# One PSUM bank per projection unit from the seventh on, the last x block asked for earlier, the folded weights later

## The chip, the core and the metric

The kernel runs on one core of a Trainium2 chip. The metric is the device time of one execution in microseconds (us), as the median of several runs. The core has five engines that each run their own instruction stream in order and meet through semaphores: TensorE (PE) for matmuls, VectorE (DVE), ScalarE (ACT), GpSimd (POOL), and SyncE (SP), which here only issues DMA transfers. Matmuls write to PSUM, which has eight banks of 128 partitions x 512 float32; ACT and DVE read it from there.

## The reference

Two attention branches read the same x (2048 tokens, width 448, 16 heads of 28), and a gate per token mixes their outputs:

```python
g = sigmoid((x * gate_w).sum(-1, keepdims=True))
a = A_ref(x, A_wqkv, A_w_phi, A_wo)   # linear attention, Hedgehog feature map
b = B_ref(x, B_wqkv, B_wo)            # softmax attention
return g * a + (1 - g) * b

# A: q, k, v = split(x @ wqkv)
pq, pk = q @ w_phi, k @ w_phi                       # per head
phi_q = concat([softmax(pq), softmax(-pq)])         # phi_k the same of pk
num = phi_q @ (phi_k^T @ v); den = phi_q @ sum(phi_k) + 1e-6
a = (num / den) @ wo

# B: q, k, v = split(x @ wqkv)
p = softmax(q @ k^T * 28**-0.5)
b = (p @ v) @ wo
```

## The kernel before

All matmuls take float32 operands that are split into a high part (rounded to the PE's fp32r format) and a low part (the rest); a product is the sum of high x high, high x low and low x high. The last of the four 128-row blocks of x and of its weights holds only 64 rows, and its other 64 rows carry the low part, so that a projection takes 11 matmuls: three for each of the first three blocks, two for the last (`x3`, L110).

The part that the change touches is the front of the kernel: the q and k projection of branch B. `UNITS` (L554) lists 28 units (m, t): m is a block of 128 of the 896 q and k columns, t a block of 512 of the 2048 tokens. Units 0 to 3 (t = 0) are computed together in `first_units` (L605), as their inputs arrive. Units 4 to 19 follow one by one in the loop at L646, and the last eight are spread over the next stage. `proj_qk` (L559) takes a PSUM bank, runs the 11 matmuls, and `keep_qk` (L568) evicts the result: ACT writes the high part into a tile `ev` (four buffers in rotation), DVE subtracts it to get the low part, and SP stores both to the scratch tensor `qk_d` in DRAM.

A unit's bank comes from `later` as long as that list has entries, then from `ps_s`, a rotation of three single banks (tag "s"; units 0 to 2 hold them first). The entries of `later` are halves of two pair tiles `pr[0]` and `pr[1]` from `ps_mx` (two banks each, tag "mx"), which the max units use later on.

What else goes on in that loop, by the unit number n:

- x comes in four blocks of 512 tokens. `x_loads(t)` issues two transfers of two 128-row blocks each into staging tiles (`stg`, three buffers in rotation, which the weights' loads share); `splits(n + 1)` calls `split_x`, in which ACT writes the high part of both halves to `XH`, and DVE and POOL the low parts. Block 2 is split at n=4, block 3 at n=8, each ahead of that unit's own eviction. The units of block 3 begin with n=12.
- `phi` and the transposed k weights of branch A (`wkAT`, four transfers, `load_fold` at L375) are loaded; `fold` (L382) multiplies them, eight small matmuls for each of four groups, into a bank of the same `ps_s` rotation, and ACT and DVE evict the result into `wkA_s`. `load_fold` begins with a one-row copy on POOL that reads `phi_s` and orders the loads behind it. All four folds are needed by the first `pk` projection of the next stage.
- `wB1`, the weights of units 16 and up, is loaded at n=10 and split at n=12 and n=14.
- `pair_query` and `pair_load` read parts of `qk_d` back (tiles qp, kp, kt; ten transfers for the first pair); POOL forms differences of the keys from them (`take_subs`, at n=14 and 19). From n=16 on `mx_unit` (L258), which looks for the largest score of each query, runs ahead of each unit: four small matmuls into two pair tiles, one ACT and two DVE instructions.

PE, DVE, ACT and POOL run in the order in which the program writes their instructions. The order of SP's queue is set by a planner that picks among the transfers that it expects to be ready, the earlier in the program first; so SP's order can differ from the program's.

Of the kernel before, what the change touches and what calls it, by code (L numbers as in the profile page):

```python
# [34 lines left out]
def f32(ap):  # L35
    return ap.bitcast(F32)
# [3 lines left out]
def gated_mix_kernel(ctx, tc, xT, wqkB, wvB, wvA, wkAT, wqAT, phi, woA, woB,  # L40
# [20 lines left out]
    def ps_s(nm):  # L61
        return ps.tile([P, 512], F32, tag="s", name=nm, bufs=psn[0])

    def ps_pv(nm):
        return ps.tile([P, 512], F32, tag="pv", name=nm, bufs=1)

    def ps_mx(nm, d):
        return ps.tile([P, 2, 512], F32, tag="md" if d and psn[1] == 3 else "mx", name=nm,
                       bufs=1 if d and psn[1] == 3 else 2)
# [29 lines left out]
    def weights(place, nm):  # L99
        if place == 1:  # L100
            return wp.tile([P, 2, 4, 512], F32R, tag="w1", name=nm)
        if place == 2:
            return front.tile([P, 2, 4, D], F32R, tag="w2", name=nm)
        return wp.tile([P, 2, 4, 450], F32R, tag="w3", name=nm)
# [31 lines left out]
    def take_lows():  # L136
        while lows:
            lows.pop(0)()
# [25 lines left out]
    def take_acts():  # L164
        while acts:
            acts.pop(0)()

    def take_subs():
        while subs:
            subs.pop(0)()  # L170
# [35 lines left out]
    def pair_load(g, c):  # L206

        hp, b = divmod(c, 2)
        heads = (2 * hp, 2 * hp + 1)
        r = mx_tile("kc", f"kp{g}_{c}", 5)  # L210
        t = mx_tile("kd", f"kt{g}_{c}", 1)
        mx_rows(r, (0, 1), k_d[g], heads, b * 1024)
        mx_rows(r, (2, 3), k_d[g], heads, b * 1024 + 512)
        mx_rows(t, (2, 3), k_d[g], heads, b * 1024)
        mxs[("kp", g, c)] = r

        def sub():
            for i in (2, 3):
                js = slice(32 * i, 32 * i + DH)
                nc.gpsimd.tensor_sub(r[js], f32(r[js]), f32(t[js]))  # L220

        subs.append(sub)

    def pair_query(gq, hp):
        g, qb = divmod(gq, NQ)
        mxs[("qp", gq, hp)] = mx_rows(mx_tile("qc", f"qp{gq}_{hp}", 3), range(4), q_d[g],
                                      (2 * hp, 2 * hp + 1) * 2, qb * 512)
# [127 lines left out]
    def load_x(t, b):  # L355
        return stage(2, 512, xT[:, b:b + 2, t * 512:(t + 1) * 512], f"xraw{t}_{b}")
# [18 lines left out]
    def load_fold(src, nm):  # L375
        wts[nm] = bk.tile([112, NG, 512], F32, tag="wt", name=f"wt{nm}", bufs=1)
        if nm == "k":
            nc.gpsimd.tensor_copy(wts[nm][:1, :, 0], phi_s[:1, :, 0])
        for k in range(NG):
            nc.sync.dma_start(wts[nm][:, k, :], src[:, k, :])  # L380

    def fold(dst, nm, g, b0=0, n=4):  # L382

        wt = wts[nm][:, g, :]
        pw = ps_s(f"pw{nm}{g}_{b0}")
        for b in range(n):
            nc.tensor.matmul(pw[:, b * 112:(b + 1) * 112], wt[:, (b0 + b) * P:(b0 + b + 1) * P],
                             phi_s[:, g, :], start=True, stop=True)
        pw3 = pw[:, :n * 112].rearrange("p (b f) -> p b f", f=112)
        bs, gs = slice(b0, b0 + n), slice(g * 112, (g + 1) * 112)  # L390
        nc.scalar.copy(dst[:, 0, bs, gs], pw3)
        nc.vector.tensor_sub(dst[:, 1, bs, gs], pw3, f32(dst[:, 0, bs, gs]))
# [166 lines left out]
    def proj_qk(n, ev):  # L559

        m, t = UNITS[n]
        tt = slice(t * 512, (t + 1) * 512)
        pq = later.pop(0) if later else ps_s(f"pqk{t}_{m}")
        w, c = wB[m // 4], m % 4 * P
        run(pq, [(w[:, i, b, c:c + P], x) for b, x, i in x3(tt)])
        keep_qk(m, t, pq, ev)

    def keep_qk(m, t, pq, ev):  # L568
        tt = slice(t * 512, (t + 1) * 512)
        e = ev.tile([P, 2, 512], F32R, tag="ev", name=f"ev{t}_{m}")  # L570
        nc.scalar.copy(e[:, 0, :], pq)  # L571
        nc.vector.tensor_sub(e[:, 1, :], pq, f32(e[:, 0, :]))  # L572
        nc.sync.dma_start(qk_d[m * P:(m + 1) * P, :, tt], f32(e))
# [7 lines left out]
    wkA_s = weights(2, "wkA_s")  # L581
# [3 lines left out]
    def loads(key, *fns):  # L585
        raws[key] = [f() for f in fns]

    def x_loads(t):
        loads(("x", t), lambda: load_x(t, 0), lambda: load_x(t, 2))

    def part_loads(key, src, n, nm):
        loads(key, lambda: load_part(src, n, nm, 0), lambda: load_part(src, n, nm, 2))

    def split_part(w, key, n, i, low=nc.vector):
        split_weight(w, raws[key][i], slice(2 * i, 2 * i + 2), slice(0, n), low)

    def splits(n):

        if n % 4 == 1 and n < 12:
            split_x(n // 4 + 1, raws.pop(("x", n // 4 + 1)))  # L600
        if n in (13, 15):
            split_part(wB[1], "wB1", 384, (n - 13) // 2)
        take_lows()

    def first_units():  # L605

        raw = [stg.tile([P, 2, 512], F32, tag="stg", name=f"first_raw{b}") for b in range(3)]
        raw.append(f32(ev.tile([P, 2, 512], F32R, tag="ev", name="first_raw3")))
        for b in range(4):
            nc.sync.dma_start(raw[b][:, 0, :], wqkB[:, b, :512])  # L610
            nc.sync.dma_start(raw[b][:, 1, :], xT[:, b, :512])
        x_loads(1)
        pqs = [ps_s(f"pqk0_{m}") for m in range(3)] + [ps_pv("pqk0_3")]
        pr = [ps_mx(f"pqk_{i}", False) for i in range(2)]
        later.extend((pr[0][:, 0, :], pr[1][:, 0, :], pr[0][:, 1, :]))
        for _ in range(8):
            nc.tensor.matmul(pqs[3][:, :P], ident, ident, start=True, stop=True)
        for b in range(4):
            w, x = wB[0][:, :, b, :], XH[:, b, :512]
            nc.scalar.copy(w[:, 0, :], raw[b][:, 0, :])  # L620
            (nc.scalar.copy if b else nc.vector.tensor_copy)(x, raw[b][:, 1, :])
            nc.vector.tensor_sub(w[:, 1, :], raw[b][:, 0, :], f32(w[:, 0, :]))
            if b < 3:
                nc.vector.tensor_sub(XL[:, b, :512], raw[b][:, 1, :], f32(x))
                todo = [(0, x), (1, x), (0, XL[:, b, :512])]
            else:
                nc.vector.tensor_sub(x[64:], raw[b][64:, 1, :], f32(x[64:]))
                todo = [(0, x), (1, x)]
            if b < 3:
                order = [(i, m) for i in range(3) for m in range(4)]  # L630
            else:
                order = [(i, m) for m in range(4) for i in range(2)]
            for i, m in order:
                nc.tensor.matmul(pqs[m], w[:, todo[i][0], m * P:(m + 1) * P], todo[i][1],
                                 start=b == 0 and i == 0, stop=b == 3 and i == 1,
                                 skip_group_check=True)
        hold = raws[("x", 1)][0][:1, 0, :4]
        splits(1)
        nc.gpsimd.tensor_copy(phi_s[:1, :, 0], hold)
        for m in range(4):  # L640
            keep_qk(m, 0, pqs[m], ev)

    later = []
    first_units()
    pkv = ps_pv("pkv")
    for n in range(4, NP):  # L646
        take_acts()
        if n in (4, 6):
            x_loads(n // 2)
        if n == 5:  # L650
            nc.sync.dma_start(phi_s, phi)
            load_fold(wkAT, "k")
        if n == 10:
            part_loads("wB1", wqkB[:, :, 512:896], 384, "wB1")
        splits(n + 1)
        if n == 14:
            part_loads("wvA", wvA, 450, "wvA")
            nc.sync.dma_start(sel_s, sel)
            nc.sync.dma_start(mask_s, mask)
            for v in vap:  # L660
                nc.gpsimd.memset(v[:, :, 28:32], 0.0)
                nc.gpsimd.memset(v[:, :, 28:29], 1.0)
        if 16 <= n < 20:
            mx_unit()
        proj_qk(n, ev)
        if n in (16, 18):
            split_part(wvA_s, "wvA", 450, (n - 16) // 2)
            take_lows()
        if n in (10, 12, 14, 17):
            fold(wkA_s, "k", {10: 0, 12: 1, 14: 2, 17: 3}[n])  # L670
        if n == 10:
            pair_query(0, 0)
            pair_load(0, 0)
        if n == 15:
            pair_load(0, 1)
            pair_query(0, 1)
        if n in (14, 19):
            take_subs()
# [522 lines left out]
```

## Time and profile before

| | us |
|---|---|
| median of 3 runs | 1028.66 |
| lowest and highest of them | 1027.72 and 1028.92 |
| span of the profiled execution | 1027.1 |
| PE busy in it | 1018.7 (99%) |
| ACT busy in it | 819.4 (80%) |
| DVE busy in it | 672.8 (65%) |
| POOL busy in it | 245.1 (24%) |

The span runs from the first to the last instruction of one execution, the slowest (here the only) core's. PE's busy time is that of pipelined matmuls, so that 99% does not mean that PE works at its peak. PEld is PE's weight load, which overlaps its matmuls. In rows of waits, "A <- B: 2.3, 1, 2.3" says that A's engine sat idle for 2.3 us in total, once, at longest 2.3 us, until B ended. In rows of the timeline, neighbouring instructions of one kind are merged ("x4"), and their durations overlap where they are pipelined. "SPq" rows are the issuing of a transfer by SP, not the transfer itself.

### The profile page before, as it was taken

The page shows a single profiled execution, that of the slowest core. Times are in us where ns is not written, and L with a number is a line of the kernel's source. Part 1 is how long each engine was busy: PE and PEld are TensorE (multiplying, and loading weights), DVE is VectorE, ACT ScalarE, POOL GpSimd, SP SyncE. Part 2 cuts the span into 40 slices and gives each one's busy share as a digit, 9 for nine tenths or more (in the row PEclk, how much of TensorE's full clock was granted, in tenths as well). Part 3 has the DMA queues.
Part 4 walks back from the last instruction along what each step waited for, and adds up shares of the span by engine and source line. Part 5 has one row for each costly group of instructions (what it writes and reads, how often), then busy time and mean ns, then how long its engine had stood idle before and what let it go on. Part 6 is the DMA issues. An engine that isn't in the chain of part 4 may idle for free.

```text
span 1027.1 us, 17751 instructions
## 1 busy us (share of the span) xinstructions
PE 1018.7 (99%) x6344; PEld 561.2 (55%) x6344; DVE 672.8 (65%) x1335; ACT 819.4 (80%) x1534; POOL 245.1 (24%) x213
## 2 busy tenths in 40 slices
PE   8999999999999999999999999999999999999998
PEld 7878888878779433333333333333333333354545
DVE  5466566997750578888878788787878887710102
ACT  5354445687753899999999999999999999969672
POOL 1226456688436302111011110101201101011010
PEclk9999999999999999999999999999999999999999
DMA  8873110132245703233633123522313355414311
GB/s 294 292 243 116 42 34 19 43 90 79 91 129 122 158 19 83 65 71 68 127 70 77 46 66 81 129 57 50 87 46 74 87 131 138 124 56 127 122 42 54
DMA packets 64025, 98.88 MB, mean 96 GB/s; under 512 B 17952, under 2 KB 24720, under 8 KB 63936
## 3 DMA queue, kind: packets, MB, share of 16 engines
q1 hardware_dynamic: 63936, 97.74, 35.4%
q8 instruction: 50, 0.82, 0.4%
q14 instruction: 39, 0.32, 0.1%
HBM read 69.54 MB, written 27.78 MB: 95 GB/s over the span
## 4 chain that ended last, share of the span: by engine, by line
PE 95%; DVE 2%; DMA 1%; ACT 1%; issue 0%; SPq 0%; DVEq 0%; ACTq 0%
PE st L850 29%; PE pv L977 25%; PE pm L321 9%; PE pqk L108 5%; PE poa L108 4%; PE pk L126 4%; PE pva L126 4%; PE pob L108 3%; PE pq L108 3%; PE pvb L108 2%; PE pmb L284 2%; PE pvb L126 2%; PE pn L532 1%; PE pft L520 1%; PE pkv L475 1%; PE poL L1011 1%
## 5 line engine op out<-in xcount | busy, mean ns | idle before, releaser
L868 ACT ACTIVATE p<-st 128x512 f32<-128x512 f32 x1020 | 525.9, 609 | 29.5 <-PE st L850 27.8
L332 DVE TENSOR_REDUCE part<-pm 128x1 f32<-128x512 f32 x477 | 304.6, 685 | 131.5 <-PE pm L321 124.9
L850 PE MATMUL st<-qst,kst 128*128 128x512 f32 x1024 | 315.6, 430 | 0.5 <-ACT vb L694 0.5
L977 PE MATMUL pv<-p,vb 128*32 128x512 f32 x2048 | 272.8, 605 | 0.2 <-DVE oUb L398 0.2
L850 PEld LDWEIGHTS st<-qst,kst 128*128 128x128 f32 x1024 | 173.1, 187 | 137.4 <-issue 75.8
L321 PEld LDWEIGHTS pm<-kc,qc 28*128 28x128 f32 x848 | 40.5, 181 | 177.8 <-ACT p L868 169.4
L325 ACT ACTIVATE rl<-pm 128x512 f32<-128x512 f32 x212 | 126.9, 599 | 11.1 <-PE pm L321 0.3
L419 POOL TENSOR_TENSOR oUb<-oUb,rsb 128x512 f32<-128x512 f32 x15 | 19.4, 1291 | 469.2 <-DMA rsb<-rdb 375.1
L329 DVE CUSTOM_DVE_ANT_0 rl<-pm,rl 128x512 f32<-128x512 f32 x159 | 108.2, 680 | 0.0
L321 PE MATMUL pm<-kc,qc 28*128 28x512 f32 x848 | 107.1, 495 | 0.0
L289 DVE CUSTOM_DVE_ANT_0 rl<-pmb,rl 128x512 f32<-128x512 f32 x88 | 57.1, 686 | 32.4 <-ACT rl L287 32.4
L977 PEld LDWEIGHTS pv<-p,vb 128*32 128x32 f32 x2048 | 40.3, 108 | 67.6 <-issue 63.4
L988 DVE SCALAR_TENSOR_TENSOR acc<-pob,gate,acc 128x448 f32<-128x448 f32 x12 | 8.2, 683 | 86.2 <-PE pob L108 86.2
L108 PE MATMUL pqk<-XH,wB 128*128 128x512 f32 x192 | 60.8, 404 | 2.3 <-DVE ev L572 2.3
L287 ACT ACTIVATE rl<-pmd 128x1024 f32<-128x1024 f32 x44 | 45.3, 1029 | 8.0 <-ACT z_s L485 2.4
L571 ACT CAST ev<-pqk 128x512 fp32r<-128x512 f32 x28 | 16.0, 589 | 40.2 <-PE pqk L108 35.7
L108 PE MATMUL poa<-woA_s,oTa 128*128 128x448 f32 x192 | 43.2, 374 | 0.0
L108 PEld LDWEIGHTS pqk<-XH,wB 128*128 128x128 f32 x192 | 36.0, 192 | 11.4 <-DVE ev L572 2.7
L572 DVE TENSOR_TENSOR ev<-pqk,ev 128x512 fp32r<-128x512 f32 x28 | 19.0, 690 | 31.6 <-ACT ev L571 31.5
L108 PEld LDWEIGHTS poa<-woA_s,oTa 128*128 128x128 f32 x192 | 35.0, 188 | 5.8 <-issue 2.8
L195 POOL TENSOR_TENSOR kc<-kc,kd 28x512 fp32r<-28x512 f32 x12 | 15.4, 1282 | 95.7 <-DMA kc<-qkd 59.4
L126 PE MATMUL pk<-wkA_s,XH 128*128 128x448 f32 x128 | 37.9, 377 | 0.0
(155 smaller groups left out, 1186.6 us busy)
## 6 DMA issues: line engine op xcount, KB each, us to landing
qkd<-ev SPq DMA_DIRECT2D x28, 512.0 KB
qst<-qkd SPq DMA_DIRECT2D x64, 224.0 KB
kst<-qkd SPq DMA_DIRECT2D x64, 224.0 KB
od<-oTb SPq DMA_DIRECT2D x48, 112.0 KB
rsa<-rda SPq DMA_DIRECT2D x8, 512.0 KB
rsb<-rdb SPq DMA_DIRECT2D x15, 256.0 KB
kc<-qkd SPq DMA_DIRECT2D x64, 56.0 KB
gad<-ga SPq DMA_DIRECT2D x16, 224.0 KB
```

The costliest lines, as they stand in the source:

```text
L108: nc.tensor.matmul(dst, l, r, start=i == 0, stop=i == len(todo) - 1)
L126: nc.tensor.matmul(dst[:, :n], l, r, start=i == 0, stop=i == len(todo) - 1, skip_group_check=True)
L284: nc.tensor.matmul((pb if j < 2 else pd)[:, j % 2, :], qc[js, qt * P:(qt + 1) * P], kc[js, :], start=True, stop=True, tile_position=(32 * ...
L287: nc.scalar.activation(rl, pd, AF.Relu)
L289: nc.vector.tensor_tensor_reduce(rl[:, i, :], pb[:, i, :], rl[:, i, :], 1.0, LOWEST, ALU.add, ALU.max, part[:, col + i:col + i + 1])
L321: nc.tensor.matmul(pm[j], mxs[("qc", gq)][js, qt * P:(qt + 1) * P], mxs[("kc", g, kb)][js, :], start=True, stop=True, tile_position=(32 * ...
L325: nc.scalar.activation(rl, pm[kb], AF.Relu if kb < 3 else AF.Copy)
L329: nc.vector.tensor_tensor_reduce(r, pm[j], r, 1.0, LOWEST, ALU.add, ALU.max, part[:, col + j:col + j + 1])
L332: nc.vector.tensor_reduce(part[:, col + j:col + j + 1], pm[j], AX.X, ALU.max)
L850: nc.tensor.matmul(st, kst_of[(g, kt // 4)][:, j, (kt % 4) * P:(kt % 4 + 1) * P], qst_of[gq][:, j, :], start=True, stop=True)
L868: nc.scalar.activation(p, st, AF.Exp, scale=SCALE)
L977: nc.tensor.matmul(pv[32 * j:32 * j + 32, :], vb[kt // 8][:, kt % 8, 4 * g + j, :], pt[j], start=kt == 0, stop=kt == NT - 1, tile_position ...
```

## The change

Three edits, all in the front.

```diff
@@ first_units
         pqs = [ps_s(f"pqk0_{m}") for m in range(3)] + [ps_pv("pqk0_3")]
         pr = [ps_mx(f"pqk_{i}", False) for i in range(2)]
-        later.extend((pr[0][:, 0, :], pr[1][:, 0, :], pr[0][:, 1, :]))
+        later.extend((pr[0][:, 0, :], pr[1][:, 0, :]))
@@ the loop over units 4 to 19
-        if n in (4, 6):
-            x_loads(n // 2)
-        if n == 5:
+        if n in (4, 5):
+            x_loads(n - 2)
+        if n == 8:
             nc.sync.dma_start(phi_s, phi)
             load_fold(wkAT, "k")
...
-        if n in (10, 12, 14, 17):
-            fold(wkA_s, "k", {10: 0, 12: 1, 14: 2, 17: 3}[n])
+        if n in (13, 15, 17, 18):
+            fold(wkA_s, "k", {13: 0, 15: 1, 17: 2, 18: 3}[n])
```

Units 4 and 5 keep the first halves of the two pair tiles. The seventh unit (n=6) took the second half of the first pair and now takes a bank of the `ps_s` rotation, so that each later user of this rotation moves on by one. Block 3 of x is loaded at n=5 instead of n=6; `phi` and the k weights of branch A at n=8 instead of n=5; and the four folds run at n=13, 15, 17 and 18 instead of 10, 12, 14 and 17. No instruction is added or taken away.

## The prediction

> **What bounds the kernel now.** I read the page first: the span, the 40 slices and the chain that ended last.
>
> ```profile
> span 1027.1 us, 17751 instructions
> ...
> DMA  8873110132245703233633123522313355414311
> ...
> PE 95%; DVE 2%; DMA 1%; ACT 1%; issue 0%; SPq 0%; DVEq 0%; ACTq 0%
> ```
>
> TensorE (PE) is the chain for 95% of the span, so a microsecond (us) taken off PE's stream early should reach the end, unless a later wait eats it. The DMA engines are full only in the first three slices, some 77 us, and there the change lies. So I next took the waits of PE over the whole span, and those of SyncE's (SP's) DMA queue up to 130 us.
>
> ```profile
> PE pqk L108 <- DVE ev L572: 2.3, 1, 2.3
> ...
> PE pmd L284 <- DVE part L289: 0.6, 2, 0.3
> ```
>
> ```profile
> SPq L573 <- DVE ev L572: 50.2, 15, 14.0
> ```
>
> The first is PE's longest single wait. SP mostly stands waiting for evictions whose result it is to store, and everything behind such a store in its queue waits along. The timeline places PE's wait (start, duration, engine; the bracket is the idle time before it and what ended it):
>
> ```profile
> 19.91 0.39 PE L108 MATMUL pqk<-XL,wB 128*128 128x512 f32 x1
> 20.14 0.61 PE L108 MATMUL pqk<-XH,wB 128*128 128x512 f32 x2
> 23.04 1.01 PE L108 MATMUL pqk<-XH,wB 128*128 128x512 f32 x2 [2.29 <-DVE ev L572]
> ...
> 26.79 1.09 PE L108 MATMUL pqk<-XH,wB 128*128 128x512 f32 x4
> ```
>
> ```profile
> 21.68 0.59 ACT L571 CAST ev<-pqk 128x512 fp32r<-128x512 f32 x1 [3.29 <-DMA qkd<-ev]
> 22.97 0.59 ACT L571 CAST ev<-pqk 128x512 fp32r<-128x512 f32 x1 [0.71 <-DMA qkd<-ev]
> ```
>
> ```profile
> 15.42 2.48 DVE L572 TENSOR_TENSOR ev<-pqk,ev 128x512 fp32r<-128x512 f32 x4
> 17.82 1.21 DVE L365 TENSOR_TENSOR XL<-xraw,XH 128x1024 fp32r<-128x1024 f32 x1
> ...
> 22.30 0.69 DVE L572 TENSOR_TENSOR ev<-pqk,ev 128x512 fp32r<-128x512 f32 x1 [1.54 <-ACT ev L571]
> ```
>
> Unit 6 (n=6 of the loop at L646) starts at 23.04, as VectorE (DVE) ends unit 4's eviction at 22.99. Unit 4 sits in the first half of the pair that unit 6 takes the second half of. That eviction was late because its output buffer (4 in rotation) waited until 21.6 for unit 0's store to land. The wait has a second price, seen in the windows of time (length, busy times with counts, granted clock, DMA share, GB/s):
>
> ```profile
> 23.04:27.24 4.20, 4.20 (x11) 3.30 (x12) 0.69 (x1) 0.52 (x1) 0.00 (x0) 0.59 0.86 260
> 27.24:29.76 2.52, 2.52 (x12) 2.06 (x11) 0.69 (x1) 0.59 (x1) 0.00 (x0) 1.00 0.88 263
> 24.00:25.00 1.00, 1.00 (x4) 0.81 (x3) 0.28 (x1) 0.00 (x0) 0.00 (x0) 0.50 0.90 328
> 20.60:47.53 26.93, 24.64 (x110) 20.36 (x110) 10.55 (x16) 9.64 (x16) 2.83 (x11) 0.94 0.87 295
> ```
>
> After the wait the granted clock is 0.50, and unit 6 takes 4.20 us where unit 7 takes 2.52.
>
> **The change part by part.** *The single bank.* Matmuls start 0.23 us apart (19.91 to 20.14), so unit 6 could start at 20.14 + 2 x 0.23 = 20.60. Its new place is the bank of unit 0, whose eviction is the first of the four DVE ones that run from 15.42 to 17.90. It is free well before 20.60. Removed: 23.04 - 20.60 = 2.44 us of wait, and 4.20 - 2.52 = 1.68 us of slow clock; together 4.12 us.
>
> The Trainium skill, "TensorE: Matmul & The Clock Gate", Part 1, says that the clock drops only after an idle window of about 3.4 us, whose phase runs free of the kernel. This trace shows 0.50 after a gap of 2.3 to 2.4 us; by the rule read strictly the slow stretch is not the gap's, and only 2.44 us would go.
>
> What is late next: unit 6's own eviction. It needs the buffer of unit 2's store. Units 0 and 1 landed at 21.6 and 22.9, 1.3 us apart; by the same step units 2 and 3 land near 24.2 and 25.5 (estimate). Unit 6 ends at 20.60 + 2.52 = 23.1, so ScalarE (ACT) waits about 1.1 us, and DVE is done near 25.5. Its bank is wanted by unit 9, at 20.60 + 3 x 2.52 = 28.2. Cover 2.7 us: cost nothing. Unit 7 likewise against unit 10.
>
> *The last x block and the weights to be folded* trade places in SP's queue:
>
> ```profile
> 11.67 0.42 SPq L658 DMA_DIRECT2D sel_s<-in_sel_dram  x1
> 13.37 2.46 SPq L131 DMA_DIRECT2D xraw<-in_xT_dram  x2
> 16.39 7.14 SPq L573 DMA_DIRECT2D qkd<-ev  x5
> 23.62 2.97 SPq L380 DMA_DIRECT2D wtk<-in_wkAT_dram  x4
> 26.68 0.52 SPq L573 DMA_DIRECT2D qkd<-ev  x1
> 27.25 0.61 SPq L131 DMA_DIRECT2D xraw<-in_xT_dram  x1
> ...
> 38.83 1.20 SPq L573 DMA_DIRECT2D qkd<-ev  x1
> 40.08 2.88 SPq L175 DMA_DIRECT2D qp<-qkd  x4
> ...
> 45.10 0.81 SPq L175 DMA_DIRECT2D kt<-qkd  x2
> 46.00 2.61 SPq L573 DMA_DIRECT2D qkd<-ev  x3
> 48.71 2.08 SPq L131 DMA_DIRECT2D wvA_raw<-in_wvA_dram  x2
> ```
>
> ```profile
> qkd<-ev SPq DMA_DIRECT2D x22, 512.0 KB
> ...
> wtk<-in_wkAT_dram SPq DMA_DIRECT2D x4, 224.0 KB
> ```
>
> ```profile
> 34.13 1.05 ACT L361 CAST XH<-xraw 128x1024 fp32r<-128x1024 f32 x1 [2.59 <-DMA xraw<-in_xT_dram]
> 35.09 1.07 ACT L571 CAST ev<-pqk 128x512 fp32r<-128x512 f32 x2
> ```
>
> Six x transfers: the fifth already goes out at 13 to 16 us, only the sixth (second half of block 3) sits at 27.25, behind the five stores, the four weight loads and unit 5's store. It lands at 34.1, and ACT stands 2.59 us for it, with unit 8's eviction queued behind. Before, that cost PE nothing. With PE 4.1 us earlier, unit 11 (which in the new rotation takes unit 8's bank) starts at 20.60 + 5 x 2.52 = 33.2. The load's staging buffer is free at 19.03 (the DVE row at 17.82), so it can go out right after unit 4's store, near 23.6, with the weights' 4 x 224 KB and unit 5's 512 KB no longer ahead: 1.4 MB, which at the 295 GB/s of the last window is 4.9 us. Landing: 34.1 - 4.9 = 29.2. Then ACT takes 1.05 and 0.59 and DVE its 0.69: unit 8's bank is free near 31.7. Cover 1.5 us: cost nothing; bounds 0 and, with no earlier landing, the wait of rival B.
>
> The weights, now at n=8, go behind three or four more stores. They are wanted by the first fold, moved to n=13: after 8 units, 20.60 + 20.2 = 40.8. Before, that fold ran unhindered at 37.24, with the loads issued from 23.62. Even if they go out 6 us later they have as long as before, less 2 us. GpSimd's (POOL's) small copy ahead of them keeps its place in POOL's queue. Cost nothing.
>
> *The four folds* move, none goes. One costs PE 0.88 us (chain of waits), shown with its neighbours:
>
> ```profile
> 37.41 0.88 PE pwk L387 x8
> ```
>
> ```profile
> 37.24 1.04 PE L387 MATMUL pwk<-phi_s,wtk 112*128 112x112 f32 x8
> ...
> 52.56 0.50 PE L284 MATMUL pmb<-kp,qp 28*128 28x512 f32 x2
> ...
> 66.23 0.51 PE L284 MATMUL pmb<-kp,qp 28*128 28x512 f32 x2
> 67.06 0.49 PE L284 MATMUL pmd<-kp,qp 28*128 28x512 f32 x2 [0.33 <-DVE part L289]
> ```
>
> The last fold now stands right behind unit 18 on ACT and DVE, ahead of the reductions that the max unit at 66.23 waits for (0.83 us to 67.06). Those come about 0.6 us later, PE 0.88 us later: between a gain of 0.3 and a loss of 0.3; I take 0.
>
> *The new wait.* Only two folds, not three, now stand ahead of the first max unit (n=16). It moves from 52.56 to 20.60 + 10 x 2.52 + 2 x 0.88 = 47.6. It needs key differences made on POOL:
>
> ```profile
> 47.53 3.25 POOL L220 TENSOR_TENSOR kp<-kp,kt 28x512 fp32r<-28x512 f32 x2 [9.41 <-DMA kt<-qkd]
> ```
>
> These start as kt lands (47.53) and take 3.25: done at 50.78, 1.8 us of slack before. Now they must start by 44.3. The landing follows SP: unit 10's store at 38.83, 1.59 after unit 10's matmuls (37.24), and kt 8.70 after that. Unit 10 now ends at 33.2, which gives 33.2 + 1.59 + 8.70 = 43.5. The DMA engines set a floor: they were 0.87 busy from 20.60 to 47.53, so 3.5 us were idle, and the same bytes cannot land before 44.0. The ceiling is the old 47.53. So the wait lies between 0 and 50.78 - 47.6 = 3.2 us; SP's path points near the floor, and I take a landing of 45.1, a wait of 0.8. A wait this short (0.33 us at 67.06 against 2.29 at 23.04) I take without the clock's price. Behind it on PE stands unit 16, whose eviction nobody is short of.
>
> *Sum:* 1027.1 - 4.12 + 0.8 = 1023.8 us for the profiled execution. The median stands 1.56 us above its span (1028.66 - 1027.1), so 1025.3.
>
> **The rivals.** *B, x lands no earlier:* SP's order keeps the sixth x load behind the weights. Landing 34.13 as before, unit 8's bank free as DVE ends near 36.6; unit 11 waits 36.6 - 33.2 = 3.4 us and, as after the 2.29 us wait, pays 1.68: 4.12 - 5.1 = -1.0, 1029.6. For it: SP's order is not the program's (sel, asked for at n=14, went out at 11.67). Against: nothing but program position holds the load.
>
> *C, the transfers are the bound:* kt lands at the old 47.53. The max unit waits 3.2, plus 1.68: 1029.4. For it: 0.87 busy DMA engines. Against: 3.5 us of idle.
>
> *D, slower:* the pair loads (qp, kp, kt) slip behind the next three stores and the wvA loads in SP's queue. From 46.00 to 50.79 these hold SP 4.8 us: kt at 45.1 + 4.8 = 49.9, differences at 53.2, a wait of 5.6 and 1.68 on top: 4.12 - 7.3 = -3.2, 1031.8. It decides from a landing of about 46.7 on, where wait and clock together reach 4.1. For it: SP stood 50.2 us behind stores, and any change of timing may reorder it. Against: program order puts the pair loads first.
>
> *E, the slow clock comes anyway,* if its phase and not the gap makes it: 1028.66 - 2.44 + 0.8 = 1027.0. Against: the slow stretch begins with the first matmuls after the gap, and unit 5's before it are 0.23 us apart. This is the result that the Trainium skill's 3.4 us window gives.
>
> That unit 6 waits in its new bank too I rule out by the row at 15.42.
>
> **How the numbers follow.** Forecast 0.66 (1024.2 to 1026.6: new waits of 0 to 2 us, 0.3 either way for the fold); B 0.08; C 0.10; D 0.12; E 0.04. The range 1024.0 to 1029.8 leaves out D and little else. About 0.2%, 2 us, is what can be told from no change: faster is below 1026.6, nearly all of the forecast, 0.63; B, C, E and its edge lie within, 0.25; slower is D, 0.12.
>
> **What would show it.** Right: unit 6 starts near 20.6 with no gap, 11 matmuls in 2.5 us at clock 1.00; the x row of ACT lands before 30; the first max unit at 47.6 to 49.6. Wrong: a gap of over 2 us before unit 11 (B) or the first max unit (C, D) and a clock of 0.50 behind it, or 0.50 with no gap (E). If the matmuls of the row at 67.06 run 3 us earlier and the span is no shorter, the gain was lost later, and I have missed the place.

## The result, and the profile after

| | before | after |
|---|---|---|
| median of 21 runs each, us | 1028.22 | 1026.57 |
| lowest and highest | 1026.90, 1029.13 | 1025.95, 1028.68 |
| ratio to before, 95% interval | | 0.9985 (0.9980 to 0.9991) |
| span of the profiled execution | 1027.1 | 1026.9 |

By the ratio the change makes the kernel 0.15% faster, 1.5 us (the two medians lie 1.65 us apart): the forecast direction, within the range, and less than half of the 3.3 us that the sum gave. It lies inside the 0.2% that I had called "same". That the median, 1026.57, still falls just inside the forecast's 1024.2 to 1026.6 is luck: that band was reckoned from the 1028.66 of three runs, and the 21 runs put the kernel before at 1028.22. The two spans show even less, 0.2 us; the profiled execution of the changed kernel happens to be the slowest of its 21 (1028.68), so that the spans must not be set against each other. The traces can be, stretch by stretch.

PE's waits over the whole span, after (total, times, longest):

```profile
...
PE pmd L284 <- DVE part L289: 1.0, 3, 0.5
PE pq L108 <- DVE ev L572: 0.8, 1, 0.8
PE pqk L108 <- DVE ev L572: 0.6, 1, 0.6
```

The 2.3 us wait is gone, and two smaller ones are new: one for a projection unit (0.6) and one for a `pq` (0.8), which no step of the prediction had. PE's timeline after places them:

```profile
20.31 1.07 PE L108 MATMUL pqk<-XH,wB 128*128 128x512 f32 x4
...
22.80 1.07 PE L108 MATMUL pqk<-XH,wB 128*128 128x512 f32 x4
...
42.32 0.73 PE L108 MATMUL pqk<-XH,wB 128*128 128x512 f32 x2 [0.56 <-DVE ev L572]
...
48.41 0.50 PE L284 MATMUL pmb<-kp,qp 28*128 28x512 f32 x2
...
55.68 0.50 PE L284 MATMUL pmb<-kp,qp 28*128 28x512 f32 x2
56.47 0.50 PE L284 MATMUL pmd<-kp,qp 28*128 28x512 f32 x2 [0.28 <-DVE part L289]
...
63.73 0.51 PE L284 MATMUL pmb<-kp,qp 28*128 28x512 f32 x2
64.22 0.50 PE L284 MATMUL pmd<-kp,qp 28*128 28x512 f32 x2
```

The rows "x4" hold the last two matmuls of one unit and the first two of the next. So unit 6 runs from about 20.8, without a gap, 22.80 - 20.31 = 2.49 us long. Unit 14 waits at 42.32. The first max unit starts at 48.41. The last row here answers to 67.06 before: PE is 2.84 us ahead there.

What the other engines did (ACT, POOL, SP's queue, and the window of the same bounds as before):

```profile
24.80 0.59 ACT L571 CAST ev<-pqk 128x512 fp32r<-128x512 f32 x1 [0.66 <-DMA qkd<-ev]
...
29.76 1.05 ACT L361 CAST XH<-xraw 128x1024 fp32r<-128x1024 f32 x1 [2.19 <-DMA xraw<-in_xT_dram]
...
39.84 0.83 ACT L142 CAST wB<-wB_raw 128x768 fp32r<-128x768 f32 x1 [3.33 <-DMA wB_raw<-in_wqkB_dram]
40.58 1.06 ACT L571 CAST ev<-pqk 128x512 fp32r<-128x512 f32 x2
...
53.12 0.95 ACT L142 CAST wvA_s<-wvA_raw 128x900 fp32r<-128x900 f32 x1 [0.82 <-DMA wvA_raw<-in_wvA_dram]
```

```profile
44.75 2.65 POOL L220 TENSOR_TENSOR kp<-kp,kt 28x512 fp32r<-28x512 f32 x2 [11.01 <-DMA kt<-qkd]
```

```profile
23.30 0.60 SPq L131 DMA_DIRECT2D xraw<-in_xT_dram  x1
24.89 2.99 SPq L573 DMA_DIRECT2D qkd<-ev  x3
27.98 3.23 SPq L380 DMA_DIRECT2D wtk<-in_wkAT_dram  x4
```

```profile
20.60:47.53 26.93, 26.36 (x121) 21.84 (x120) 11.59 (x16) 10.25 (x16) 5.25 (x12) 1.00 0.96 334
```

SP's order came out as forecast: the x load behind unit 4's store, the weights behind unit 7's. The x half lands before 29.76. But the DMA engines are now 0.96 busy where they were 0.87, and the load of wB1's first half lands only at 39.84. ACT stands 3.33 us for it, and unit 12's eviction behind it comes too late for unit 14, which takes its bank. Before the change ACT came to the same split later, and had nothing to wait for:

```profile
41.34 0.84 ACT L142 CAST wB<-wB_raw 128x768 fp32r<-128x768 f32 x1
```

So ACT now wants this load 4.8 us sooner (39.84 - 3.33 = 36.51), and SP sends it out 1.6 us later (33.51 for 31.92). How much of the wait is due to these two, and how much to the busier DMA engines, no run separates.

The third `pq` projection, first before and then after:

```profile
185.58 0.99 PE L475 MATMUL pkv<-featk,vap 128*32 128x56 f32 x64
186.50 0.68 PE L108 MATMUL pq<-wqA_s,XH 128*128 128x448 f32 x2
```

```profile
182.68 0.99 PE L475 MATMUL pkv<-featk,vap 128*32 128x56 f32 x64
184.48 0.47 PE L108 MATMUL pq<-wqA_s,XH 128*128 128x448 f32 x1 [0.81 <-DVE ev L572]
```

Into this place PE comes 2.90 us ahead, out of it 2.02. A later max unit, before and after:

```profile
283.35 0.50 PE L284 MATMUL pmd<-kp,qp 28*128 28x512 f32 x2
```

```profile
282.29 0.50 PE L284 MATMUL pmd<-kp,qp 28*128 28x512 f32 x2 [0.50 <-DVE part L289]
```

Here PE is 1.06 us ahead, and by the spans 0.2 at the end: another 1.8 us are lost behind `pq` in this one execution. Whether that belongs to the change is a question for the experiments.

### The profile page after: what moved, and what is told of

Its sections match the earlier page's. It is cut to its first block, busy times and chain, and to the rows that moved or that the text cites. A ratio compares the mean times of both kernels' runs of the same rounds, so it can differ in the third digit from the quotient of the medians.

```text
span 1026.9 us, 17749 instructions
## 1 busy us (share of the span) xinstructions
PE 1018.9 (99%) x6344; PEld 561.2 (55%) x6344; DVE 671.0 (65%) x1335; ACT 819.3 (80%) x1534; POOL 243.5 (24%) x213
## 4 chain that ended last, share of the span: by engine, by line
PE 92%; DMA 4%; DVE 3%; ACT 1%; issue 0%; SPq 0%; POOL 0%; ACTq 0%; POOLq 0%; DVEq 0%
PE st L850 29%; PE pv L977 25%; PE pm L321 9%; PE pk L126 4%; PE pva L126 4%; PE poa L108 4%; PE pob L108 3%; PE pq L108 2%; PE pqk L108 2%; DMA qkd<-ev 2%; PE pvb L126 2%; PE pmb L284 1%; PE pvb L108 1%; PE pft L520 1%; PE pn L532 1%; DMA gad<-ga 1%
## 5 line engine op out<-in xcount | busy, mean ns | idle before, releaser
L108 PE MATMUL pq<-wqA_s,XH 128*128 128x448 f32 x128 | 37.3, 374 | 0.8 <-DVE ev L572 0.8
```

Source lines behind the costliest of these rows:

```text
L108: nc.tensor.matmul(dst, l, r, start=i == 0, stop=i == len(todo) - 1)
```

## The experiments

**One part alone.** Three kernels split the change. The first has only the bank:

```diff
-        later.extend((pr[0][:, 0, :], pr[1][:, 0, :], pr[0][:, 1, :]))
+        later.extend((pr[0][:, 0, :], pr[1][:, 0, :]))
```

> The bank edit alone; x loads, weights and folds as before. Theory: the wait ahead of unit 6 (2.44 us) and its slow clock (1.68 us) go, but the sixth x transfer still sits behind the weights in SP's queue and lands near 34, so that unit 8's eviction waits for it on ScalarE, and unit 11, which takes unit 8's bank, waits some 3 us for that with the slow clock behind: first pk 0 to 2 us earlier than in the kernel before, time within 0.1% of it. Rival (the loads' order does not matter): no wait at unit 11, first pk at least as early as in the changed kernel (64.65 us).

Measured: median 1031.28, ratio 1.0023 (1.0012 to 1.0034), slower than before. PE's timeline, and ACT's row for the last x half:

```profile
32.72 0.61 PE L108 MATMUL pqk<-XH,wB 128*128 128x512 f32 x2
36.80 1.66 PE L387 MATMUL pwk<-phi_s,wtk 112*128 112x112 f32 x8 [3.46 <-issue]
...
68.34 0.49 PE L284 MATMUL pmd<-kp,qp 28*128 28x512 f32 x2 [0.33 <-DVE part L289]
```

```profile
34.21 1.04 ACT L361 CAST XH<-xraw 128x1024 fp32r<-128x1024 f32 x1 [6.78 <-DMA xraw<-in_xT_dram]
```

The wait that was removed comes back at another place: the x half lands at 34.2, as before the change, ACT stands 6.78 us for it, and unit 8's bank is not free. With the folds still at n=10, it is the first fold that takes this bank, so that the fold waits, not unit 11 as I had written. (Its row names no releaser; DVE ends unit 8's eviction near 36.7.) The wait is 3.46 us and a step of slow clock follows it; rival B had priced them at 3.4 and 1.68. The theory's mechanism held, but its "within 0.1%" was too kind: the late wait costs more than the one removed, PE comes to the first `pk` 1.3 us later than before, and the `pq` wait of 0.8 us is in this kernel too. Of its 12 runs, 9 have a mean clock of 0.998 or less.

The second has the loads and folds moved and the bank kept:

```diff
-        if n in (4, 6):
-            x_loads(n // 2)
-        if n == 5:
+        if n in (4, 5):
+            x_loads(n - 2)
+        if n == 8:
...
-        if n in (10, 12, 14, 17):
-            fold(wkA_s, "k", {10: 0, 12: 1, 14: 2, 17: 3}[n])
+        if n in (13, 15, 17, 18):
+            fold(wkA_s, "k", {13: 0, 15: 1, 17: 2, 18: 3}[n])
```

> The loads and folds moved as in the change, the third entry of the list of banks kept. Theory: unit 6 still waits about 2.3 us at a clock of 0.5 behind it, the other moves are worth nothing by themselves: time within 0.1% of before. And since the rotation of single banks is as before, pq at about 186 us has no wait for DVE. Rival (the loads are what helped): 1.5 us faster than before with unit 6 still waiting.

Measured: median 1029.54, ratio 1.0009 (1.0000 to 1.0018): worth nothing by itself. There is no wait for `pq` at 186 us. What I had not expected is in the wait itself:

```profile
19.59 0.61 PE L108 MATMUL pqk<-XH,wB 128*128 128x512 f32 x2
23.39 0.74 PE L108 MATMUL pqk<-XH,wB 128*128 128x512 f32 x2 [3.19 <-DVE ev L572]
```

A longer wait than before, 3.19 us, and no slow clock behind it (below, under the clock). That holds for this one execution: of the 11 runs, 9 have a mean clock of 0.998 or less. PE also stands longer at the max units here, 1.5 us in all against 0.6.

The third has the bank and the earlier x load; the weights and the folds stay as in the kernel before:

> The bank edit and the earlier x load, weights and folds as in the kernel before. Theory: the x load goes out ahead of the four weight loads, lands before 31, and fold 0 at n=10 (33 us), which takes unit 8's bank, waits at most 1 us; first pk within 1 us of the changed kernel's. Rival (the weights' later place is needed too): fold 0 waits over 1.5 us for unit 8's eviction, with a window of slow clock in part of the runs, and the time is no better than before.

Measured: median 1029.47, ratio 1.0001 (0.9992 to 1.0009). The rival holds for the time, with another wait than it named:

```profile
35.58 0.73 PE L108 MATMUL pqk<-XH,wB 128*128 128x512 f32 x2 [1.44 <-DVE ev L572]
```

```profile
23.98 2.27 SPq L380 DMA_DIRECT2D wtk<-in_wkAT_dram  x4
26.35 9.71 SPq L573 DMA_DIRECT2D qkd<-ev  x5
```

Fold 0 runs on time; unit 11 behind it waits 1.44 us for unit 9's eviction. The weights' 0.9 MB now go out ahead of the stores of units 5 and up, whose landing frees the eviction buffers; that this is what keeps unit 9's eviction on ACT until 34.21 is argued, not shown, as its row names another releaser. Of the 11 runs, 7 have a mean clock of 0.998, a slow step. The `pq` wait of 0.8 us is in this kernel as well. So the bank is not enough alone, nor with the earlier x load: the weights and folds have to go later too. Whether the earlier x load is still needed then, and which of weights and folds counts, no run separates.

**What the old wait was for.** In the kernel before, unit 6 is given the second half of the other pair:

```diff
-        later.extend((pr[0][:, 0, :], pr[1][:, 0, :], pr[0][:, 1, :]))
+        later.extend((pr[0][:, 0, :], pr[1][:, 0, :], pr[1][:, 1, :]))
```

> The kernel before, with unit 6 in the second half of the second pair instead of the first. Theory (the wait is for the reader of the same pair tile, not for a bank): unit 6 now waits for unit 5's eviction and starts as that ends on DVE, about 1.3 us later than in the kernel before, near 24.3 us; where the pause fills most of one 3.41 us step of the clock, a slow step of 3.41 us follows; time 1 to 2 us above before. Rival (a bank clash or something else on PE): unit 6 starts at 23.0 as before.

Measured: median 1032.16, ratio 1.0031 (1.0018 to 1.0044).

```profile
23.93 1.22 PE L108 MATMUL pqk<-XH,wB 128*128 128x512 f32 x2 [3.58 <-DVE ev L572]
```

```profile
23.18 0.69 DVE L572 TENSOR_TENSOR ev<-pqk,ev 128x512 fp32r<-128x512 f32 x1 [0.60 <-ACT ev L571]
```

Unit 6 starts 0.06 us after unit 5's eviction ends (23.87), whose half it does not touch. The wait is for the readers of the tile, both halves as one. The time grew more than expected: two slow steps follow in the profile, not one, and four of the five runs have a mean clock of 0.997 or less.

**The clock.** Each run lists its mean granted clock; one slow step of 3.41 us costs 1.7 us where PE is busy all through it, and brings the mean to 0.998. Of the 77 runs of the kernel before that stood beside the experiments, 32 show 0.998 or less. So the slow step that I took off in full is met in four executions of ten, if it is the wait ahead of unit 6 that makes it in each of them; only the profiled one shows where it lies. And these 32 runs are 0.93 us slower on average than the other 45 (1029.12 against 1028.19), not 1.7. What the others lose in its place is open, as no trace of such a run exists; a longer wait without a slow step, as in the second experiment, would do it. Windows laid on steps of 3.41 us, one kernel each (length, PE busy, ..., clock): the kernel before, the second experiment, the one with the other pair.

```profile
19.90:23.31 3.41, 1.12 (x5) 0.65 (x4) 1.55 (x2) 0.92 (x2) 0.90 (x2) 1.00 1.05 400
23.31:26.73 3.42, 3.42 (x9) 2.65 (x9) 0.69 (x1) 0.25 (x1) 0.00 (x0) 0.50 0.89 270
26.73:30.14 3.41, 3.41 (x16) 2.78 (x16) 0.69 (x1) 0.72 (x2) 0.00 (x0) 1.00 0.84 249
```

```profile
18.52:21.94 3.42, 1.68 (x8) 1.06 (x6) 1.58 (x1) 0.00 (x0) 1.63 (x2) 1.00 1.05 397
21.94:25.35 3.41, 1.96 (x8) 1.61 (x9) 1.38 (x2) 1.17 (x2) 0.00 (x0) 1.00 0.88 333
```

```profile
19.14:22.55 3.41, 1.21 (x6) 0.67 (x4) 1.54 (x2) 0.58 (x1) 0.93 (x2) 1.00 1.05 407
22.55:25.96 3.41, 2.03 (x5) 1.65 (x6) 0.72 (x2) 0.58 (x1) 0.00 (x0) 0.50 0.96 314
25.96:29.38 3.42, 3.42 (x10) 2.64 (x9) 0.00 (x0) 0.36 (x1) 0.00 (x0) 0.50 0.87 218
```

In the clock records of the traces, each change lies a whole number of steps of 3.413 us behind the first one of its execution (5 in the kernel before, from 6.25 to 23.31; 9 with the bank alone). The step just over decides. With 1.12 and 1.21 us of PE's work in a step at full clock, the next one is slow; with 1.68 and 1.96 it is not. The slow step of the third kernel at 22.55 held 2.03 us of work, and the next one is slow all the same: at half the clock that is about what PE does in 1.0 us at full clock (an estimate), so busy time alone may not be what counts. The 3.19 us wait is cut in two by a step's end, and each part leaves its step half busy; the 2.29 us wait falls into one step and fills two thirds of it. Where the steps fall relative to the kernel differs from one execution to the next: in three traces of the changed kernel a step ends at 44.27, at 43.91 and at 42.41.

**The `pq` wait.** The idea was that the rotation of single banks stands one place further on after the change. When the pool is opened anew ahead of the third `pq`, its first bank would then be the one that the last projection unit (unit 27) still holds. The first attempt:

```diff
             psn[0] = 4
+            ps_s("pad")
```

> The changed kernel, with one bank of the rotation left out, unused, when the pool of PSUM banks is opened anew ahead of the third pq projection. Theory: the 0.81 us wait of that pq for the eviction of the last projection unit (at 184 us, not there in the kernel before) comes from the rotation standing one place further on after the change, so that the first bank of the new pool is the one evicted last; with one bank left out the wait goes, and the time is 0.8 us under the changed kernel's (about 0.08%). Rival (DVE is simply late there): the wait stays or moves to the next bank with the same length.

Measured: median 1027.05, ratio 0.9986 (0.9977 to 0.9994), with the 0.81 us wait still there, now at 185.22. It told nothing of the theory: a bank that nobody uses is not placed, and in the built program `pq` stayed in unit 27's bank (no profile shows the banks). So this run is the changed kernel once more. Its `pq` starts 186.50 - 185.22 = 1.28 us ahead of before, and its span (1025.8) is 1.3 us shorter. The second attempt restores the rotation instead:

```diff
-        later.extend((pr[0][:, 0, :], pr[1][:, 0, :]))
+        later.extend((pr[0][:, 0, :], pr[1][:, 0, :]))
+        half[9] = pr[0][:, 1, :]
...
-        pq = later.pop(0) if later else ps_s(f"pqk{t}_{m}")
+        pq = half.pop(n) if n in half else later.pop(0) if later else ps_s(f"pqk{t}_{m}")
```

> The changed kernel, with unit 9 (not unit 6) in the second half of the first pair, so that the rotation of single banks stands from unit 10 on as in the kernel before. The bank left out in the earlier run had no effect, since an unused bank is not placed; in the programs as built, the third pq and the last projection unit lie in the same bank in the changed kernel and in different banks in the kernel before. Theory: unit 4's eviction is long done when unit 9 starts at 28 us, no new wait there, and the 0.81 us wait at 184 us goes; pq then runs 2.9 us ahead of the kernel before instead of 2.1, and the time is about 0.8 us (0.08%) under the changed kernel's, ratio to before 0.9975 to 0.998. Rival (DVE is late in any case): the wait stays.

Measured: median 1026.71, ratio 0.9982 (0.9974 to 0.9991).

```profile
182.75 0.99 PE L475 MATMUL pkv<-featk,vap 128*32 128x56 f32 x64
183.67 0.68 PE L108 MATMUL pq<-wqA_s,XH 128*128 128x448 f32 x2
```

No wait: `pq` follows 0.92 us after the start of the row ahead of it, as in the kernel before (186.50 - 185.58), and is 2.83 us ahead of it. The span is 2.3 us shorter than before's. In the times the step can't be told from the changed kernel's (intervals overlap); in the trace it is plain. And over all twelve traces, the six kernels with the shifted rotation (the changed one and its two repeats, the bank alone, the bank with the x load, and the later split below) have this wait of 0.8 us, the six others have none. So the shifted rotation is shown to be the cause.

**The new wait ahead of unit 14.** The split of wB1's first half is put behind unit 12's eviction:

```diff
-        if n in (13, 15):
-            split_part(wB[1], "wB1", 384, (n - 13) // 2)
+        if n in (14, 15):
+            split_part(wB[1], "wB1", 384, n - 14)
```

> The changed kernel, with the first half of wB1 split one unit later (n=13 instead of 12). Theory: the new 0.56 us wait ahead of unit 14 is unit 12's eviction standing on ScalarE behind a split whose load lands only at 39.8 us; with the split behind that eviction the wait goes and nothing takes its place, first max unit at 47.6 to 47.9 us instead of 48.41, time 0.5 us under the changed kernel's if it carries. Rival (the transfers are the bound there): a wait of about the same length comes at the next unit or at the first max unit.

Measured: median 1028.03, ratio 0.9994 (0.9985 to 1.0002), worse than the changed kernel if anything. The wait ahead of unit 14 is gone, and the rival is right:

```profile
48.79 0.50 PE L284 MATMUL pmd<-kp,qp 28*128 28x512 f32 x1 [0.84 <-POOL kp L220]
```

```profile
46.14 2.60 POOL L220 TENSOR_TENSOR kp<-kp,kt 28x512 fp32r<-28x512 f32 x2 [12.82 <-DMA kt<-qkd]
```

PE reaches the first max unit earlier (47.00) and stands there for the key differences, since kt landed at 46.14. In the three traces of the changed kernel it landed at 44.75, 44.94 and 45.76, so part of this wait may belong to the one execution. Of the 11 runs, 7 show 0.998. Which gap gave them their slow step no trace shows; the profiled execution has none.

**Both together, and work put into the gap.** With unit 9's bank and the later split as above, the third fold runs right behind the second, ahead of the first max unit:

```diff
-        if n in (13, 15, 17, 18):
-            fold(wkA_s, "k", {13: 0, 15: 1, 17: 2, 18: 3}[n])
+        for g in {13: (0,), 15: (1, 2), 17: (3,)}.get(n, ()):
+            fold(wkA_s, "k", g)
```

> The former, with the first half of wB1 split at n=13 instead of 12 and the folds at n=13, 15, 15 and 17: the third fold fills the time in which the first max unit would wait for its key differences, the fourth no longer stands ahead of the last reductions. Theory: no wait ahead of unit 14 and at most 0.3 us at the first max unit; first pk about 3.4 us ahead of before instead of 2.8, and 0.5 us off the time. Rival (the transfers are the bound there): the waits come back elsewhere between 40 and 65 us, and the first pk is no earlier than in the changed kernel (64.65).

Measured: median 1026.14, ratio 0.9973 (0.9962 to 0.9984). Then once more beside the changed kernel on one chip:

> The changed kernel once more, beside the kernel before and the next one on one chip. Theory: no step of slow clock in any of its runs, in about half of those of the kernel before; ratio to before 0.9975 to 0.999; in the profile the third pq waits 0.8 us at about 184 us and PE is about 2.1 us ahead of the kernel before from there to the end, with no loss between 265 and 295 us as the first profile had it. Rival: the losses between 265 and 295 us come again, and belong to the change.

> The combined version once more: ratio to before 0.996 to 0.9985 and below that of the changed kernel beside it by 0.0005 to 0.0015, if what it gained before is its own; rival: the two cannot be told apart.

| on one chip | median us | ratio to before, 95% interval | runs at a clock of 0.998 |
|---|---|---|---|
| before | 1028.31 | | 6 of 17 |
| changed | 1027.07 | 0.9988 (0.9979 to 0.9997) | 4 of 11 |
| combined | 1025.26 | 0.9973 (0.9963 to 0.9984) | 0 of 7 |

The combined version is the fastest of all, and its gain came again; of the 11 runs of the changed kernel beside it, only two lie as low as its slowest (1025.96). That "no slow step" would be seen in the changed kernel was wrong. Its profiled execution here has one:

```profile
43.45 0.84 PE L108 MATMUL pqk<-XH,wB 128*128 128x512 f32 x2 [1.84 <-DVE ev L572]
```

```profile
40.97 0.83 ACT L142 CAST wB<-wB_raw 128x768 fp32r<-128x768 f32 x1 [4.60 <-DMA wB_raw<-in_wqkB_dram]
```

```profile
40.50:43.91 3.41, 1.57 (x12) 1.32 (x11) 2.08 (x4) 2.94 (x5) 0.00 (x0) 1.00 0.75 282
43.91:47.33 3.42, 3.42 (x10) 2.67 (x9) 1.48 (x3) 0.03 (x1) 1.50 (x2) 0.50 0.65 231
```

The same program waits 0.56 us ahead of unit 14 in one execution and 1.84 in another, as wB1's load lands at 39.84 or at 40.97. With 1.57 us of work in the step, a slow one follows: against the 1.68 of the second experiment this puts the boundary near one half. This execution ends with before's span (1027.1), its `pq` wait of 0.8 included. The losses behind `pq` did not come again, here or in the repeat under the first `pq` attempt: both end by as much ahead of before as they leave `pq` (0.0 here, 1.3 there). They belonged to the one execution, 0.8 of the 1.8 us at the max unit shown; the rest is not traced. In the combined version, the folds fill that time:

```profile
47.04 1.94 PE L387 MATMUL pwk<-phi_s,wtk 112*128 112x112 f32 x16
48.91 0.50 PE L284 MATMUL pmb<-kp,qp 28*128 28x512 f32 x2
...
64.01 0.49 PE L284 MATMUL pmd<-kp,qp 28*128 28x512 f32 x2 [0.47 <-DVE part L289]
```

No wait stands ahead of the first max unit, and the last one is 67.06 - 64.01 = 3.05 us ahead of before. That is 0.2 us better than the changed kernel's first profile, not the 0.6 expected; in the first combined run PE stood 0.7 us for kp all the same. What the version gains beyond that is, as far as these rows show, the `pq` wait and the slow step that none of its 13 runs has.

## Why the prediction was right, and where its sizes were off

*The single bank:* right. Unit 6 runs at once, its eviction begins on ACT at 24.80 (24.2 was worked out), and nobody waits for it. The 2.44 us of wait are gone. The term of 1.68 us is the one most off: it stood in the profiled execution that I read, but not in all. At 32 of 77 runs it is worth at most 1.68 x 0.42 = 0.7 us on average, one whole microsecond less, and by the times of these runs 0.93 x 0.42 = 0.4. I read a chance of the execution as a property of the kernel; the spread of the runs before (1027.72 to 1028.92) could have warned me. Nor does the slow stretch begin with the first matmuls behind the gap, as I held against rival E: it begins at 23.31, at a step's end, 0.27 us after unit 6 does.

*The last x block and the weights:* right, with a landing at 29.76 for the worked out 29.2. (From there unit 8's bank is free at 31.5, not 31.7, by the rows that I added up; nothing hangs on it.) The first part alone showed that this cover was needed, and rival B's price of 5.1 us was that of a kernel without it: the last max unit's row there, at 68.34, is 1.28 us behind before's where unit 10 still ended 4.06 ahead (32.72 + 2 x 0.23 = 33.18, against 37.24). That is 5.3 us lost between the two places.

*The folds:* 0, within 0.3 either way. The last one's wait fell from 0.83 to 64.22 - 63.73 = 0.49, a gain of 0.3, the edge of what was allowed. But the max unit of n=18 now waits 56.47 - 55.68 = 0.79 (1.02 and 0.01 in the two other traces of this program), which the sum did not have: the split of wvA stands on ACT until its load lands (53.12), ahead of ACT's part of the max unit of n=17.

*The new wait:* the size came out by luck, the place and the cause were wrong. The sum had the first max unit at 47.6 + 0.8 = 48.4; it started at 48.41, but at 48.89 and 51.17 in the two other traces of this program. kt landed at 44.75 (45.1 taken), POOL needed 2.65 us instead of 3.25, and the differences were ready in time. Of the 0.8 us, 0.56 had been lost earlier, ahead of unit 14, and 0.17 ahead of unit 6, which began at 20.77 instead of 20.60. I had named the cover of units 6 to 11 and looked no further for loads of later stages in ACT's queue. Rival C named a cause that fits, DMA engines without slack (0.96 busy), but at another load.

*What had no step:* the `pq` wait, 0.81 us, at 184 us. I had written that each later user of the rotation moves on by one, and followed this to unit 11, not to the place where the pool is closed and opened anew.

*The sum by what the runs showed:* 2.4 of wait off (3.3 in the second experiment, where the same wait stands: 19.59 + 2 x 0.23 to 23.39) and 0.4 to 0.7 of clock, against 0.6 to 1.9 ahead of unit 14, 0.5 at the max units, 0.8 at `pq`, and 0.2 for a slow step of 1.7 in 4 of the 43 runs of this program. That is between a loss of 0.6 and a gain of 1.9 us; the three ratios of this program (0.9985, 0.9986, 0.9988) say 1.2 to 1.5. The sizes agree no better than that: each term here comes from one to three executions. Taken whole, the three traces of this program are 2.02, 1.28 and 0.03 us ahead of the one trace of before as they leave `pq`, 1.1 on average.

The rivals: D did not come, the pair loads kept their place. E as written fell, as the clock had no slow step in the first trace after; but gap and phase decide together, and its 1027.0, which leaves the 1.68 us out, lies nearer to the measured 1026.57 than the 1025.3 of the sum. The chances were too sure of the size: 0.63 for a gain of over 0.2%, and the result, 0.15%, fell to the 0.25.

## What to carry to other kernels

Here, a wait that was removed from a stage that the transfers almost fill came back in part at the next load in some engine's queue. So list every load that stands ahead of an eviction up to the point where the transfers slacken, and put spare work of PE where the last one stands. Read a term off several executions before it is taken in full, above all a slow clock: the mean clock of each run tells how often it is paid, and the times of these runs what it costs. And an edit that adds or takes one place in a rotation of buffers shifts every later user, here up to where the rotation is handed over to another pool.

## What the runs showed of the hardware that was not expected

The clock drops for a whole step of 3.41 us, and the steps run on their own: in the traces here the slow stretches are 23.31 to 26.73, 43.91 to 47.33, and 22.55 to 29.38 as two in a row. The Trainium skill, "TensorE: Matmul & The Clock Gate", Part 1, has the length (3413 ns) and that the window runs free of the kernel, and the traces agree (3.413 us, and ends of steps at 44.27, 43.91 and 42.41 in one program): the prediction's strict reading, by which a gap of 2.3 us could not be the cause, was wrong. The idle window of the Trainium skill need not be idle, though: steps at full clock with 1.12, 1.21 and 1.57 us of work were followed by a slow one, steps with 1.68, 1.96 and 2.29 were not, so that about half a step is the boundary in these runs. It holds for steps at full clock alone, as the slow step with 2.03 us of work was followed by another. A wait of 3.19 us can then go without a slow step in one execution, where one of 1.84 us costs 1.7 us more in another; which of the two comes is not settled by the kernel alone, as 9 of the 11 runs of the kernel with the 3.19 us wait have a mean clock of 0.998 or less. The 2.29 is that of the repeat of the changed kernel:

```profile
39.00:42.41 3.41, 2.29 (x15) 1.88 (x13) 1.25 (x2) 2.11 (x4) 0.00 (x0) 1.00 1.01 358
42.41:45.83 3.42, 3.05 (x13) 2.54 (x14) 2.31 (x4) 1.07 (x3) 0.89 (x1) 1.00 0.53 176
```
